# Eight routed experts and a dense feed-forward on one core: conversion of its weights shared out anew, w2 split at other places, one expert's rows turned earlier

## The chip, the cores and the metric

The kernel runs on one core of one Trainium2 chip. The metric is the device time of one execution in microseconds (us). Engines are named as in the profile: PE is the matrix engine (PEld its weight loads), DVE the vector engine, ACT the scalar engine, POOL the GpSimd engine, SP the queue that issues most DMAs.

## The reference

Three layers follow each other: a recurrent attention (mLSTM), a mixture of eight experts of which each token takes one, and a dense feed-forward with a leaky ReLU.

```python
def _attn_ref(q, k, v, i_gate, f_gate, o_gate):      # B, H, S, D = 4, 8, 768, 40
    for t in range(S):
        m_new = np.maximum(f_gate[:, :, t] + m, i_gate[:, :, t])
        f_stab = np.exp(f_gate[:, :, t] + m - m_new)
        i_stab = np.exp(i_gate[:, :, t] - m_new)
        m = m_new
        C = f_stab[:, :, None, None] * C + i_stab[:, :, None, None] * np.einsum('bhd,bhe->bhde', vt, kt)
        n = f_stab[:, :, None] * n + i_stab[:, :, None] * kt
        h_tilde = np.einsum('bhde,bhe->bhd', C, qt)
        denom = np.maximum(np.abs(np.einsum('bhd,bhd->bh', n, qt)[:, :, None]), 1.0)
        y[:, :, t] = h_tilde / denom / (1.0 + np.exp(-o_gate[:, :, t]))

def _moe_ref(x, w_gate, w1, w2):                     # 3072 tokens, 320 wide, 8 experts of 1024
    logits = x @ w_gate
    expert_idx = np.argmax(logits, axis=1)
    gate_w = softmax(logits)[np.arange(N), expert_idx]
    for e in range(E):
        mask = expert_idx == e
        out[mask] = gate_w[mask, None] * (np.maximum(x[mask] @ w1[e], 0.0) @ w2[e])

def _moe2_ref(x, w_in, w_out):                       # 320 -> 2048 -> 320
    h = x @ w_in
    return np.maximum(0.01 * h, h) @ w_out
```

## The kernel before

Every float32 product is made of fp32r products: an operand is split into a high part (a cast on ACT) and a low part (the value less the high part, on DVE or POOL), and high x high, low x high and high x low are added up in PSUM. Tiles ending in h or l are such parts (`w1h`, `w1l`, `xh`, `xl`, `hh`, `hl`).

**Stage 1** (0 to about 186 us) is the attention in chunks of 128 steps, with routing: the rows of x are scattered to a DRAM buffer `xs_d`, sorted by expert (`put_rows`, L92 to L94; an indirect DMA on POOL for each 128 tokens). The scatters are placed by a table of steps: `SC4` holds the steps of the four scatters of chunk 4; those of the last chunk follow from its routing. The expert with the most tokens is picked early and called the first (e = 0); the products of its first 256 rows (`pe`) fill the end of the stage.

**Stage 2** (186 to about 404 us) runs the eight experts, e = 0 to 7, with room for 512, 512, 472, 440, 416, 384, 364 and 320 tokens. An expert is *up* (`expert_up`, eight product groups f, each of eight products through L218, then the ReLU parts `hh` on ACT at L248 and `hl` on DVE at L249) and *down* (`expert_down`, L1409: groups a = 0, 1, 2 of 24, 24 and 16 products, each with two places k = 0, 1 behind it at which other work is put in). In the places of up f the kernel splits this expert's w2 (`split_w2`: per call ACT L186, L188 and DVE L187, L189; four calls, at f = 2, 3, 5, 6). In the places of down it prepares the next expert: the rows `xr` are loaded from `xs_d` (L236, SP) once all scatters have landed, transposed on PE (L244, `x_turn`) and split (L197 ACT, L199 DVE); w1 is split in six parts (`split_w1`: ACT L164, and L165 on DVE or POOL). `xr` can be loaded only when the numbers of tokens are sorted (`counts`, DVE); the w1 and w2 loads share two buffers `raw`, so the load of w1 for the next expert waits for the splits of w2 of this one. For e = 0 the x_turn of expert 1 stands at (a, k) = (1, 1) and (2, 1), for the others at (0, 1) and (1, 1), each time behind the side work of that place.

*Side work* is the conversion of `w_in` and `w_out`, which come as 64-bit floats and are decoded to float32 parts. It is a list of 20 `pieces` (12 of w_in, "i", quarter and row block; 8 of w_out, "o", two of the 16 blocks each); a piece has five steps (`piece_step`): t = 0 issues the stores of the piece before (ACT queue) and two DVE operations; t = 1 one on ACT; t = 2 two on DVE; t = 3 one on DVE and a cast on ACT; t = 4 two subtractions on POOL (L1282, L1283). One step is taken at each place that the tables `SA` to `SH` list (0 to 7 are f in up, 8 + 2a + k in down), one table for an expert: 7, six times 7 and 13 steps, 62 in all. The first `NPRE` pieces of w_out are stored to a DRAM buffer `wo_d` and loaded again, since their final place is a buffer that w1 holds till the last up is done; `load_wo` (L1332, POOL queue, one DMA for the high and one for the low parts) brings them in at the start of the last down.

**Stage 3** (about 404 us to the end) is the dense feed-forward: two halves of the 2048 columns, six windows of 512 tokens, 96 units i of eight products `pva` and, three units later, twelve products `poa` that read `w_out` (`wo_tiles`: blocks 0 to 7 and 14 in the buffers of w1, the others in those of w2). The first half needs blocks 0 to 7. One step of side work is taken in each unit till the pieces are done: 38 units. `windows()` (some forty small DVE operations on a table of overflow windows) stands at unit 44.

The order on every engine is the order of the code; an engine waits in that order.

Of the kernel before, what the change touches and what calls it, by code (L numbers as in the profile page):

```python
# [51 lines left out]
def tile_mlstm_moe_ffn(  # L52
# [108 lines left out]
    def split_w1(raws, ws, i, eng):  # L161
        hf, a = divmod(i, 3)
        cs = slice(hf * HF, (hf + 1) * HF)
        nc.scalar.copy(ws[0][:, a, cs], raws[hf][:, a])  # L164
        eng.tensor_tensor(ws[1][:, a, cs], raws[hf][:, a], ws[0][:, a, cs].bitcast(F32), ALU.subtract)  # L165
# [16 lines left out]
    def split_w2(raws, ws, i):  # L182
        hi, lo, mx = ws
        s = slice(2 * i, 2 * i + 2)
        raw = raws[i // 2][:, (i % 2) * 2 : (i % 2) * 2 + 2]
        nc.scalar.copy(hi[:, s], raw[:, :, 0 : 2 * P])  # L186
        nc.vector.tensor_tensor(lo[:, s], raw[:, :, 0 : 2 * P], hi[:, s].bitcast(F32), ALU.subtract)  # L187
        nc.scalar.copy(mx[:, s, 0:KR], raw[:, :, 2 * P : DM])  # L188
        nc.vector.tensor_tensor(mx[:, s, KR:P], raw[:, :, 2 * P : DM], mx[:, s, 0:KR].bitcast(F32), ALU.subtract)  # L189
# [62 lines left out]
    with ExitStack() as sx:  # L252
# [264 lines left out]
        IDLE = 8  # L517
        W2N = 2
        POOLB = 3, 0, 0, 3, 4, 6, 4, 10
        SC4 = 200, 208, 205, 213  # L520
        FILL = 8, 2, 2, 2, 6
        FR = 180, 187, 190, 192
        W1S = 185, 188, 191, 206, 206, 206
# [627 lines left out]
    def list_rows(i0, i1):  # L1151
        for i in range(i0, i1):
            put_rows(list_w, (), list_d, sm_t["posi"][:, i : i + 1], sm_t["pay"][:, i])
# [145 lines left out]
                        wo_d[hl, f0:f1].rearrange("a p d -> p a d"), t.bitcast(F32).rearrange("p (a d) -> p a d", d=DM)  # L1299
                    )  # L1300

    NPRE = 2
    wo_t, wi3 = {}, []

    def wo_tiles(nm, part):
# [12 lines left out]
        return wo_t[i, 0][:, r * DM :], wo_t[i, 1][:, r * DM :], (i, f == 14)  # L1318


    pieces = [("i", qd, a) for qd in range(NQ - 1) for a in range(3)] + [("o", f2, 0) for f2 in range(NF // 4)]
    pieces += [("i", NQ - 1, a) for a in range(3)] + [("o", f2, 0) for f2 in range(NF // 4, NF // 2)]
    side_at = [0]

    def run_side(end=5 * len(pieces)):
# [24 lines left out]
    def ffn_x(xs, w, parts=range(3), n=CAP):  # L1350
        for a in parts:
            split_x(x2T[:, a, w * CAP : w * CAP + n], a, *xs)
        return xs


    def turn_ps(nm, a):
        return pm.tile([P, CAP], F32, tag="dn" if (nm, a) == (0, 2) else "tr", name=f"pt{nm}_{a}")
# [73 lines left out]
    }  # L1431
    for i in range(24):
        extras.setdefault((2 + i // 4, 2 * (i % 4) + 1), []).append(lambda i=i: list_rows(i, i + 1))
    SA = 5, 6, 7, 8, 9, 11, 13
    SB = 0, 1, 4, 6, 9, 11, 13
    SC = SD = SE_ = SF = SG = SB
    SH = 0, 1, 3, 4, 5, 6, 7, 8, 9, 10, 11, 12, 13

    SIDE = (SA, SB, SC, SD, SE_, SF, SG, SH)

    def side_work(e, i):
        if i in SIDE[e]:
            run_side()

    for e in range(E):
        last = e + 1 == E

        def in_up(f, e=e):
            global_w2 = (w2raw, w2s)
            if e and f in (2, 3, 5, 6):  # L1450
                split_w2(*global_w2, (2, 3, 5, 6).index(f))
            side_work(e, f)
            for fn in extras.get((e, f), ()):
                fn()

        hh, hl = first_up(in_up) if e == 0 else expert_up(e, xs, w1s, in_up, CAPS[e])
        if not last:
            e_r = nc.sync.value_load(slots[0:1, 0, e + 1 : e + 2], min_val=0, max_val=E - 1)
            row = nc.sync.value_load(slots[0:1, 1, e + 1 : e + 2], min_val=0, max_val=(E - 1) * NT)
            xr = x_rows_tile(e + 1)  # L1460
            x_load(xr, row, 0, CAPS[e + 1])
            w1raw = load_w1(of_expert(w1, e_r), e + 1)
            w1n = tiles_w1(e + 1)
            xs = tiles_x(e + 1)
        else:
            xf = tiles_fx("a0")

            assert 1 <= side_at[0] - 5 * (3 * (NQ - 1) + NPRE) <= 3
            wo_tiles("a", 0)
            load_wo(0, 2 * NPRE)  # L1470
        w2u = w2s

        def in_down(a, k, e=e, last=last):
            nonlocal_w = (w1raw, w1n) if not last else None
            if last and k == 1:
                ffn_x(xf, 0, (a,))
            side_work(e, 8 + 2 * a + k)
            if k == 0:
                if not last and a < 2:
                    for i in range(3):  # L1480
                        split_w1(*nonlocal_w, 3 * a + i, nc.gpsimd if i == 2 else nc.vector)
            else:

                for t in () if last else {0: (0, 1), 1: (2,)}.get(a - (e == 0), ()):
                    x_turn(turn_ps(e + 1, t), xr, xs, t, CAPS[e + 1])

        col = nc.scalar.value_load(slots[0:1, 2, e : e + 1], min_val=0, max_val=NT)
        col_v = nc.vector.value_load(slots[0:1, 2, e : e + 1], min_val=0, max_val=NT)
        expert_down(e, hh, hl, w2u, col, col_v, in_down, CAPS[e])
        if not last:  # L1490
            w1s = w1n
            w2raw, w2s = load_w2(of_expert(w2, e_r), e + 1), tiles_w2(e + 1)
# [94 lines left out]
    def ffn_side(i, k):  # L1587
        if k == 0:
            run_side()
        if (i, k) == (4, 1):  # L1590
            load_meta()
        if (i, k) == (44, 1):
            windows()

    ffn("a", list(range(NT // CAP)), tiles_wi("a"), lambda w, n: meta[:, 4 * w + n], xf, ffn_side, parts=2)
# [78 lines left out]
```

## Time and profile before

| | |
|---|---|
| time, median of 3 runs | 767.43 us (765.39 to 768.24) |
| profiled execution | 768.0 us, of which the profile's span is 766.3 us |
| PE busy | 727.3 us, 95% |
| PEld, DVE, ACT, POOL busy | 641.8, 492.2, 372.6, 255.5 us |
| mean granted clock of PE | 0.971 of 2.4 GHz |

A busy PE is not a PE at its peak: matmuls are pipelined, and the shown duration of one overlaps the next. So the places that matter are those at which a row of PE shows idle time ahead of it (in brackets, with what ended it), and the stretches in which the granted clock is 0.50, which is the lower of its two levels, 1.2 GHz.

### The profile page before, as it was taken

To read this page: it belongs to the slowest core of one execution; us is meant where nothing else is said; L and a number is where in the kernel's file an instruction comes from. 1 tells how busy PE (TensorE), PEld (TensorE's weight loads), DVE (VectorE), ACT (ScalarE), POOL (GpSimd) and SP (SyncE) were. 2 spreads that over 40 slices of the span, in tenths; PEclk is the share of its full clock that TensorE was granted. 3 is DMA by queue.
4 is the path that set the end of the run, shared out by engine and by line. 5 is a ranking of instruction groups with operands and counts; after the bars stand their busy time and mean duration, and the time that the engine had idled before them with its cause. 6 is when DMAs were issued, how large, how long until landed. Compare 5 with 4: busy or idle time off the path is not lost.

```text
span 766.3 us, 12304 instructions
## 1 busy us (share of the span) xinstructions
PE 727.3 (95%) x4226; PEld 641.8 (84%) x4226; DVE 492.2 (64%) x1066; ACT 372.6 (49%) x817; POOL 255.5 (33%) x409
## 2 busy tenths in 40 slices
PE   8998999988999999999989999999999999999992
PEld 4786878877878889999878989999999988988992
DVE  6576777875686755878686766776565455455441
ACT  4685675643445545556444555455344344344330
POOL 7556577617231433446362111112100022022022
PEclk7998999997999999999989999999999999999997
DMA  6899575343645656677657222232112022022011
GB/s 169 251 313 288 164 211 175 100 125 112 187 116 179 144 131 179 129 169 196 174 125 168 83 97 96 69 104 70 35 36 103 1 69 69 1 69 70 0 35 38
DMA packets 62834, 92.93 MB, mean 121 GB/s; under 512 B 9839, under 2 KB 43407, under 8 KB 62767
## 3 DMA queue, kind: packets, MB, share of 16 engines
q1 hardware_dynamic: 49295, 64.54, 30.4%
q10 hardware_dynamic: 9344, 18.35, 7.6%
q0 software_dynamic: 4128, 9.20, 3.8%
q8 instruction: 35, 0.57, 0.3%
q14 instruction: 32, 0.26, 0.1%
HBM read 68.09 MB, written 23.88 MB: 120 GB/s over the span
## 4 chain that ended last, share of the span: by engine, by line
PE 41%; issue 30%; DMA 9%; DVE 8%; POOL 7%; ACT 3%; SPq 1%; ACTq 0%; POOLq 0%; DVEq 0%
PE pva L218 8%; PE pu L218 8%; PE pd L1409 7%; POOL out_dram L94 3%; DMA w1r<-in_moe_w_dram 3%; PE poa L1523 3%; PE poa L1522 3%; PE poa L1521 3%; PE pI L590 2%; PE pS L556 2%; DMA xs_d<-x,dsti 2%; DMA rdo<-in_moe_w_out_dram 1%; POOL xs_d L94 1%; DMA qB<-in_qt_dram 1%; PE pD L544 1%
## 5 line engine op out<-in xcount | busy, mean ns | idle before, releaser
L218 PE MATMUL pva<-xhfa,wi 128*128 128x512 f32 x432 | 134.2, 393 | 0.4 <-DVE xhfa L199 0.4
L1566 DVE TENSOR_TENSOR lka<-pva,lka 128x512 f32<-128x512 f32 x96 | 66.3, 691 | 86.8 <-ACT lka L1565 86.3
L1565 ACT ACTIVATE lka<-pva 128x512 f32<-128x512 f32 x96 | 57.3, 597 | 98.7 <-PE pva L218 93.1
L1569 ACT CAST gha<-lka 128x512 fp32r<-128x512 f32 x96 | 59.6, 621 | 89.6 <-DVE lka L1566 89.6
L1571 DVE TENSOR_TENSOR gla<-lka,gha 128x512 fp32r<-128x512 f32 x96 | 70.1, 730 | 50.5 <-ACT gha L1569 48.1
L218 PEld LDWEIGHTS pva<-xhfa,wi 128*128 128x128 f32 x432 | 78.2, 188 | 13.3 <-DVE xhfa L199 0.8
L94 POOL DMA_INDIRECT out_dram<-ota,meta x24 | 25.3, 1053 | 186.6 <-DVE ota L1534 183.6
L547 ACT ACTIVATE E<-pD,wn 128x128 f32<-128x128 f32 x192 | 56.1, 366 | 25.6 <-PE pD L544 20.1
L218 PE MATMUL pu<-xh,w1h 128*128 128x256 f32 (+7 forms) x192 | 65.9, 345 | 1.9 <-DVE xh L199 1.7
L1523 PE MATMUL poa<-woaw1h,gla 128*128 128x320 f32 x216 | 66.8, 309 | 0.6 <-DVE gla L1571 0.6
L1522 PE MATMUL poa<-woaw1l,gha 128*128 128x320 f32 x216 | 66.7, 309 | 0.0
L1521 PE MATMUL poa<-woaw1h,gha 128*128 128x320 f32 x216 | 66.6, 308 | 0.0
L218 PE MATMUL pu<-xh,w1l 128*128 128x256 f32 (+7 forms) x192 | 65.2, 341 | 0.0
L590 PEld LDWEIGHTS pI<-nv,P 128*128 128x128 f32 x384 | 53.1, 198 | 10.4 <-DVE P L558 4.9
L590 PE MATMUL pI<-nv,P 128*128 128x123 f32 (+1 forms) x384 | 55.5, 280 | 3.5 <-DVE P L558 3.5
L218 PE MATMUL pva<-xlfa,wi 128*128 128x512 f32 x144 | 56.1, 389 | 0.0
L556 PE MATMUL pS<-qB,nK 120*128 120x384 f32 (+1 forms) x132 | 54.8, 498 | 0.0
L1409 PE MATMUL pd<-hh,w2l 128*128 128x512 f32 (+6 forms) x128 | 46.7, 365 | 2.7 <-DVE w2l L187 2.7
L1409 PE MATMUL pd<-hl,w2h 128*128 128x512 f32 (+6 forms) x128 | 46.8, 365 | 1.0 <-DVE hl L249 1.0
L1409 PE MATMUL pd<-hh,w2h 128*128 128x512 f32 (+6 forms) x128 | 47.1, 368 | 0.0
L248 ACT ACTIVATE hh<-pu 128x256 fp32r<-128x256 f32 (+7 forms) x64 | 31.7, 501 | 29.8 <-PE pu L218 24.6
L165 POOL TENSOR_TENSOR w1l<-w1r,w1h 128x512 fp32r<-128x512 f32 x14 | 20.1, 1437 | 77.3 <-ACT w1h L164 77.3
(307 smaller groups left out, 1883.7 us busy)
## 6 DMA issues: line engine op xcount, KB each, us to landing
w2r<-in_moe_w_dram SPq DMA_DIRECT2D x16, 640.0 KB
w1r<-in_moe_w_dram SPq DMA_DIRECT2D x16, 512.0 KB
xs_d<-zr SPq DMA_DIRECT2D x16, 320.0 KB
rdo<-in_moe_w_out_dram ACTq DMA_DIRECT2D x16, 320.0 KB
w1r<-in_moe_w_dram SPq DMA_DIRECT2D x32, 128.0 KB
rdi<-in_moe_w_in_dram ACTq DMA_DIRECT2D x8, 512.0 KB
no<-in_o_gate_dram SPq DMA_DIRECT2D x12, 320.0 KB
pba<-part_d SPq DMA_DIRECT2D x6, 640.0 KB
```

The lines of the kernel that those rows point to most:

```text
L218: nc.tensor.matmul(ps_t, a, b, start=start, stop=stop)
L547: nc.scalar.activation(Et[:, j], pD[:, j], AF.Exp, bias=wn[:, c, 3, HG * g + j : HG * g + j + 1])
L556: nc.tensor.matmul(pS[:, :nh], nats["K", c][:R, g], QB[p][:R, g - GCUT[p], :nh], start=True, stop=True)
L590: nc.tensor.matmul(pI[:, r0:, j], Pt[:, j], vj, start=True, stop=True)
L1409: nc.tensor.matmul(pd, aa, bb, start=(i == 0), stop=(i == len(seq) - 1))
L1521: nc.tensor.matmul(po[n], g_h[:, tsl], woh, start=(f == f0), stop=False)
L1522: nc.tensor.matmul(po[n], g_h[:, tsl], wol, start=False, stop=False)
L1523: nc.tensor.matmul(po[n], g_l[:, tsl], woh, start=False, stop=(f == f1))
L1565: nc.scalar.activation(lk, pu, AF.Copy, scale=0.01)
L1566: nc.vector.tensor_tensor(lk, pu, lk, ALU.max)
L1569: nc.scalar.copy(g_h, lk)
L1571: nc.vector.tensor_tensor(g_l, lk, g_h.bitcast(F32), ALU.subtract)
```

## The change

`NPRE` goes from 2 to 4, so all eight w_out blocks of the first half go by way of `wo_d`, and the last quarter but one of w_in moves behind them in the list of pieces: quarters 0 and 1, w_out pieces 0 to 3, quarter 2, w_out 4 and 5, quarter 3, w_out 6 and 7. The tables take 7, five times 7, 5 and 5 steps in stage 2, 52 in all; 48 are left for the units of stage 3. `split_w2` moves to f = 0, 1, 3, 4. In down, x_turn now stands ahead of the w1 splits and of the side work, and for e = 0 at (0, 0) and (1, 0). The four scatters of chunk 4 are put at step 200. `windows()` moves to unit 53.

```diff
-        SC4 = 200, 208, 205, 213
+        SC4 = 200, 200, 200, 200
...
-    NPRE = 2
+    NPRE = 4
...
-    pieces = [("i", qd, a) for qd in range(NQ - 1) for a in range(3)] + [("o", f2, 0) for f2 in range(NF // 4)]
-    pieces += [("i", NQ - 1, a) for a in range(3)] + [("o", f2, 0) for f2 in range(NF // 4, NF // 2)]
+    pieces = []
+    for qs, f2s in ((range(NQ // 2), range(NPRE)), ((2,), (4, 5)), ((3,), (6, 7))):
+        pieces += [("i", qd, a) for qd in qs for a in range(3)] + [("o", f2, 0) for f2 in f2s]
...
+    W2F = 0, 1, 3, 4
     SA = 5, 6, 7, 8, 9, 11, 13
-    SB = 0, 1, 4, 6, 9, 11, 13
-    SC = SD = SE_ = SF = SG = SB
-    SH = 0, 1, 3, 4, 5, 6, 7, 8, 9, 10, 11, 12, 13
+    SB = 2, 5, 6, 7, 9, 11, 13
+    SC = SD = SE_ = SF = SB
+    SG = 2, 5, 6, 7, 9
+    SH = 2, 5, 6, 7, 9
...
-            if e and f in (2, 3, 5, 6):
-                split_w2(*global_w2, (2, 3, 5, 6).index(f))
+            if e and f in W2F:
+                split_w2(*global_w2, W2F.index(f))
...
             load_wo(0, 2 * NPRE)
...
+            if k == (e > 0) and not last:
+                for t in {0: (0, 1), 1: (2,)}.get(a, ()):
+                    x_turn(turn_ps(e + 1, t), xr, xs, t, CAPS[e + 1])
+            if k == 0 and not last and a < 2:
+                for i in range(3):
+                    split_w1(*nonlocal_w, 3 * a + i, nc.gpsimd if i == 2 else nc.vector)
             side_work(e, 8 + 2 * a + k)
-            if k == 0:
-                if not last and a < 2:
-                    for i in range(3):
-                        split_w1(*nonlocal_w, 3 * a + i, nc.gpsimd if i == 2 else nc.vector)
-            else:
-                for t in () if last else {0: (0, 1), 1: (2,)}.get(a - (e == 0), ()):
-                    x_turn(turn_ps(e + 1, t), xr, xs, t, CAPS[e + 1])
...
-        if (i, k) == (44, 1):
+        if (i, k) == (53, 1):
             windows()
```

What stands on PE behind the first group of the first expert's down, before (`pd_0`, `pd_1` are groups a = 0 and 1, `pt` the transposes of expert 1's rows):

```order
L1409 MATMUL pd_0_3039<-hh_7_2775,w2h_2784 128x512
L1409 MATMUL pd_0_3039<-hh_7_2775,w2l_2785 128x512
L1409 MATMUL pd_0_3039<-hl_7_2783,w2h_2784 128x512
L1409 MATMUL pd_1_3078<-hh_0_2768,w2h_2784 128x512
L1409 MATMUL pd_1_3078<-hh_0_2768,w2l_2785 128x512
```

and after:

```order
L1410 MATMUL pd_0_3039<-hh_7_2775,w2h_2784 128x512
L1410 MATMUL pd_0_3039<-hh_7_2775,w2l_2785 128x512
L1410 MATMUL pd_0_3039<-hl_7_2783,w2h_2784 128x512
L244 MATMUL pt_0_3064<-ident,xr_3007 128x128 x4
L244 MATMUL pt_1_3071<-ident,xr_3007 128x128 x4
L1410 MATMUL pd_1_3092<-hh_0_2768,w2h_2784 128x512
```

The eight transposes that stood behind group 1 now stand behind group 0.

On ACT in the last expert's up, from its first ReLU part (`hh_0`) to its fifth, before (L186 and L188 split w2, L1298 stores a converted piece):

```order
L248 ACTIVATE hh_0_5022<-pu_0_5038 128x320
L248 ACTIVATE hh_1_5023<-pu_1_5051 128x320
L1298 DMA wo_d<-d_ho_0_5013 128x2x320
L1298 DMA wo_d<-rdo_0_4629 128x2x320
L248 ACTIVATE hh_2_5024<-pu_2_5070 128x320
L186 CAST w2h_5019<-w2r_0_5015 128x512
L188 CAST w2m_5021<-w2r_0_5015 128x2x64
L248 ACTIVATE hh_3_5025<-pu_3_5085 128x320
L186 CAST w2h_5019<-w2r_0_5015 128x512
L188 CAST w2m_5021<-w2r_0_5015 128x2x64
L1250 ACTIVATE d_eo_0_5064<-d_eo_0_5064,bexp 128x640
L248 ACTIVATE hh_4_5026<-pu_4_5103 128x320
```

and after:

```order
L248 ACTIVATE hh_0_5024<-pu_0_5040 128x320
L186 CAST w2h_5021<-w2r_0_5017 128x512
L188 CAST w2m_5023<-w2r_0_5017 128x2x64
L248 ACTIVATE hh_1_5025<-pu_1_5055 128x320
L186 CAST w2h_5021<-w2r_0_5017 128x512
L188 CAST w2m_5023<-w2r_0_5017 128x2x64
L248 ACTIVATE hh_2_5026<-pu_2_5072 128x320
L1214 DMA rdi_0_5083<-in_moe_w_in_dram 128x1024
L248 ACTIVATE hh_3_5027<-pu_3_5088 128x320
L186 CAST w2h_5021<-w2r_1_5019 128x512
L188 CAST w2m_5023<-w2r_1_5019 128x2x64
L248 ACTIVATE hh_4_5028<-pu_4_5105 128x320
```

Two splits of w2 now come before the third ReLU part, and the two stores ahead of it are gone from here.

On POOL at the end of the last expert's up, before (L1282 and L1283 are the subtractions of a w_out piece, `list_d` a scatter, the last two the loads of `load_wo`):

```order
L1282 TENSOR_TENSOR d_ao_0_5065<-d_ao_0_5065,d_ho_0_5136 128x640
L1283 TENSOR_TENSOR rdo_0_4804<-d_ao_0_5065,d_eo_0_5064 128x640
L93 MEMSET gap 1x1
L94 DMA list_d<-pay,posi 3072x2
L1332 DMA woaw1h<-wo_d 128x4x320
L1332 DMA woaw1l<-wo_d 128x4x320
```

and after:

```order
L1282 TENSOR_TENSOR d_ao_0_4859<-d_ao_0_4859,d_ho_0_5132 128x640
L1283 TENSOR_TENSOR rdo_0_4778<-d_ao_0_4859,d_eo_0_4858 128x640
L93 MEMSET gap 1x1
L94 DMA list_d<-pay,posi 3072x2
L1333 DMA woaw1h<-wo_d 128x8x320
L1333 DMA woaw1l<-wo_d 128x8x320
```

The order there is the same, and each of the two loads is twice as long.

## Rows read from the trace of the kernel before

**Rows 1.** Busy time by stretch: length, PE, PEld, DVE, ACT, POOL, PEclk, DMA, GB/s.

```profile
364.70:378.20 13.50, 12.69 (x75) 11.65 (x74) 7.98 (x15) 6.27 (x14) 2.71 (x2) 1.00 0.71 165
378.20:394.80 16.60, 13.42 (x88) 12.64 (x87) 14.03 (x25) 8.46 (x20) 10.53 (x10) 1.00 0.49 140
394.80:401.60 6.80, 5.82 (x22) 5.43 (x22) 5.25 (x8) 2.49 (x4) 3.43 (x5) 0.50 0.58 102
...
417.00:550.00 133.00, 133.00 (x741) 120.38 (x740) 90.27 (x135) 66.26 (x115) 23.89 (x20) 1.00 0.25 85
```

**Rows 2.** Timeline of PE, first expert: start, duration, line, [idle before, what ended it].

```profile
190.38 0.87 PE L244 MATMUL pt<-ident,xr 128*128 128x128 f32 x6 [1.94 <-DMA xr<-xs_d]
...
215.99 0.66 PE L244 MATMUL pt<-ident,xr 128*128 128x128 f32 x4 [0.65 <-DVE xl L199]
...
219.26 0.50 PE L218 MATMUL pu<-xh,w1h 128*128 128x512 f32 x1 [1.23 <-DVE xh L199]
```

**Rows 3.** Timeline of POOL, SP and DVE around 184 to 192 us.

```profile
183.37 0.96 POOL L94 DMA_INDIRECT xs_d<-x,dsti  x1 [0.22 <-issue]
...
187.34 0.37 SPq L236 DMA_DIRECT2D xr<-xs_d  x1
...
190.22 0.28 DVE L189 TENSOR_TENSOR w2m<-w2r,w2m 128x128 fp32r<-128x128 f32 x1
...
192.05 0.43 DVE L199 TENSOR_TENSOR xh<-pt,xh 64x256 fp32r<-64x256 f32 x1
```

**Rows 4.** Timeline of PE and SP in the first expert's down.

```profile
199.70 0.40 PE L1409 MATMUL pd<-hh,w2h 128*128 128x512 f32 x1
...
201.10 0.37 SPq L236 DMA_DIRECT2D xr<-xs_d  x1
...
210.61 1.03 PE L244 MATMUL pt<-ident,xr 128*128 128x128 f32 x8
```

**Rows 5.** Timeline of ACT and PE, seventh expert's down and eighth's up.

```profile
371.23 1.66 ACT L164 CAST w1h<-w1r 128x512 fp32r<-128x512 f32 x3 [5.78 <-DMA w1r<-in_moe_w_dram]
...
374.87 0.64 PE L244 MATMUL pt<-ident,xr 128*128 128x128 f32 x3 [0.81 <-DVE xl L199]
...
379.74 0.41 PE L218 MATMUL pu<-xh,w1h 128*128 128x320 f32 x1 [0.49 <-DVE xh L199]
```

**Rows 6.** Timeline of ACT, PE, POOL and DVE, eighth expert.

```profile
384.51 0.44 ACT L248 ACTIVATE hh<-pu 128x320 fp32r<-128x320 f32 x1 [2.51 <-POOL gap L93]
...
390.93 0.41 PE L1409 MATMUL pd<-hh,w2l 128*128 128x320 f32 x1 [0.52 <-DVE w2l L187]
394.24 0.41 PE L1409 MATMUL pd<-hh,w2l 128*128 128x320 f32 x1 [2.17 <-DVE w2l L187]
396.20 0.64 PE L1409 MATMUL pd<-hl,w2h 128*128 128x320 f32 x1 [0.98 <-DVE hl L249]
...
390.72 1.58 POOL L1282 TENSOR_TENSOR d_ao<-d_ao,d_ho 128x640 f32<-128x640 f32 x1 [2.30 <-ACT d_ho L1277]
...
390.80 1.65 DVE L189 TENSOR_TENSOR w2m<-w2r,w2m 128x128 fp32r<-128x128 f32 x1
```

**Rows 7.** Groups of DVE instructions, 378.2 to 394.8: count, busy us, mean ns, idle.

```profile
L249 DVE SCALAR_TENSOR_TENSOR hl<-pu,hh 128x320 fp32r<-128x320 f32 x7 | 3.4, 485 | 0.9 <-ACT hh L248 0.9
...
L187 DVE TENSOR_TENSOR w2l<-w2r,w2h 128x512 fp32r<-128x512 f32 x4 | 2.7, 682 | 0.0
```

**Rows 8.** Timeline of POOL and PE into stage 3.

```profile
396.77 0.84 POOL L1332 DMA_DIRECT2D woaw1h<-wo_d  x1
...
409.40 1.65 PE L218 MATMUL pva<-xhfa,wi 128*128 128x512 f32 x6 [0.39 <-DVE xhfa L199]
...
412.71 0.30 PE L1521 MATMUL poa<-woaw1h,gha 128*128 128x320 f32 x1
```

**Rows 9.** DMA queues, POOL's alone: packets, MB, share; 395 to 403, 403 to 407.5 us.

```profile
q0 software_dynamic: 552, 0.65, 50.0%
...
q0 software_dynamic: 534, 0.66, 58.6%
```

More of the change, by code (lines that the diff above doesn't have):

```diff
@@ L1466, in tile_mlstm_moe_ffn @@
             xf = tiles_fx("a0")
-            assert 1 <= side_at[0] - 5 * (3 * (NQ - 1) + NPRE) <= 3
+            assert side_at[0] > 5 * (3 * NQ // 2 + NPRE)
             wo_tiles("a", 0)
```

## Prediction

> **What bounds the kernel now.** I read the busy time by stretch first. In stage 3 PE shows 133.00 us busy of 133.00 at full granted clock, with a step of side work beside most units [rows 1]; nothing can be won there, so what counts is where PE still waits between 186 and 413 us. For that I read the timeline of PE for idle time in brackets and ask of each what ended it. There are five places. **A**: the first expert's remaining rows land late, 1.94 us [rows 2]. **B**: the second expert's rows are turned so late that its up waits twice, 0.65 and 1.23 us [rows 2]. **C**: between the seventh and the eighth expert, 0.81 and 0.49 us [rows 5]. **D**: in the eighth expert's down PE waits for split w2 and for hl, 0.52, 2.17 and 0.98 us [rows 6]; after the first two the granted clock falls to 0.50 (1.2 GHz) for 6.80 us [rows 1]. **E**: at the start of stage 3, 0.39 us [rows 8]. Experts 1 to 6 show no idle of PE in their ups and downs.
>
> **The sum, part by part.** It is made against the profiled execution, 768.0 us with a span of 766.3; the 1.7 us around the span and the 0.6 by which it lies over the median stay as they are.
>
> *Scatters (A).* The last of the eight scatters is issued at 183.37, and the load that waits for all of them goes out at 187.34, 3 us after that one's end [rows 3]. POOL idles ahead of these scatters, so three of chunk 4 now go out before those of the last chunk, and the last one is bound by its own routing instead, some 2.5 us earlier. The rows then land before PE has finished the idle products ahead of the transposes, and all 1.94 us of wait could go. But DVE is next: it splits w2 until 190.22 + 0.28, and only then takes the split of x, whose last piece starts at 192.05 [rows 3]. Without the wait this piece would be done at about 191.7 in place of 192.5: gain **0.8 us** (0 if the load is no earlier, 1.94 at most).
>
> *Second expert's rows (B).* Its transposes move from 210.61 to behind group 0. The 48 products from 199.70 to 210.61 take 0.227 each [rows 4], so group 0 ends at 205.15. The rows' load is issued at 201.10 [rows 4]. For half as many rows it was 3.0 us from issue to PE [rows 2, 3]; with half more of that for the doubled size, an estimate, they are there at 205.4. Both times move with A. So PE waits 0.3 us there and the 0.65 and 1.23 go: gain **1.6 us** (0 to 1.9). What is queued behind the transposes' split on ACT are the w1 casts, whose data lands later anyway; they have two groups of down as cover.
>
> *w2 sooner (C, D).* For experts 1 to 6 it moves work between places that cost PE nothing: 0, as the same four splits and the same steps stand in an up of the same length. For the seventh: w1 of the eighth lands so late that ACT idles 5.78 us for it [rows 5], and its load waits for the buffers that the w2 splits free. These are now done two places earlier, about 2.7 us at 1.33 a place; the x split is also ahead of the side work. Both waits of C go: gain **1.3 us** (0.5 to 1.3).
>
> D: before, ACT stood 2.51 us in front of the third ReLU part, since the stores ahead of it in its queue wait for POOL [rows 6]; that pushed the w2 splits to the end of up. Now DVE has in this up eight hl (0.485 each, 3.9), four w2l (0.68, 2.7) [rows 7], four w2m (0.28 [rows 3], 1.1) and three operations of side work at about 0.85 (w2l scaled to 640 columns, an estimate, 2.6): 10.3 us. It starts about 1.7 us behind PE's first product, so it ends at 12.0. PE needs the last hl with the 22nd product of down: 64 products of up and 21 more at 0.142 (0.227 scaled to 320 columns), 12.1. That is a tie; if each w2m takes 1.65 beside a POOL subtraction [rows 6], 0 to 3 us are left. I take 0.5: of 3.67 idle, **3.2 us** go (0.7 to 3.7). With no long pause the clock should stay at 1.00: half of 6.80, **3.4 us** (0 or 3.4). For comparison, 1.94 us idle in A and 1.88 in B were followed by no fall.
>
> *Fewer steps in stage 2, more in stage 3.* Ten steps (two pieces) leave the last two experts; the chain from down to stage 3 loses the side work that delayed it on DVE: **0.4 us** in E (0 to 0.4). The ten steps come to units 38 to 47. PE is 133.00 of 133.00 busy beside the same steps [rows 1], so they cost 0; DVE (90.27 of 133) is the cover. If it were gone, the four POOL subtractions could each hold PE by 1.4 us (1.65 less 0.28), 5.5. `windows()` costs 0 in unit 53 as in unit 44: no step competes with it there.
>
> *The load of w_out (F).* This is what the change adds on the path. Count from the first product of the last up, 378.20 before; the first `poa` then started 34.5 us later [rows 8]. Less the waits of C, D, E in it and the clock (0.49, 3.67, 0.39, 3.4) it is needed at 26.6, plus the 0.5 left in D, 27.1. The loads stand on POOL behind two subtractions (1.58 each [rows 6]) that follow ACT's cast in the sixth place (about 9 us), one wait for DVE and one scatter (1.3): about 14. Before, the two loads of 0.65 MB were issued from 396.77, 552 of their packets had gone by 403 and the rest by 407.5 [rows 8, 9]: 10.7 us. Twice the bytes: at the best pace that 0.66 MB in 4.5 us with its slow start allows, some 0.36 MB a us, 3.6 us more; at the mean pace 10.7 more. So the low parts land at 28.3 to 35.4, 1.2 to 8.3 too late; with the second load started sooner behind the first, in time. I take **1.5 us lost** (0 to 8.3), near the first, since the fixed part of a load isn't doubled.
>
> The page "DMA: Bandwidth & Descriptors" of the Trainium skill, section on the anatomy of one DMA on the SWDGE path, gives 2.0 us plus the bytes over 436 GB/s for such a load, and its bandwidth table advises large ones. An estimate by it: 5.0 us each, nothing lost in F, and a sum 1.5 us better, 756.7. The trace doesn't agree with it here: by it 0.65 MB would be 3.5 us, and the first load took about 6 [rows 8, 9].
>
> Sum: 0.8 + 1.6 + 1.3 + 3.2 + 3.4 + 0.4 = 10.7 less 1.5 = **9.2 us**. From 768.0 that is 758.8, from the median 767.43 it is **758.2 us**. With all gains at their upper ends and nothing lost: 1.9 + 1.9 + 1.3 + 3.7 + 3.4 + 0.4 = 12.6, 754.8.
>
> **Rivals.**
> 1. *The w_out load holds PE for long and the clock falls.* For it: D's pauses of 2.17 and 0.52 were followed by a fall [rows 1, 6], and the loads now have little slack. A wait of 4.0 in place of 1.5, and 3.4 for the clock: 767.43 - 10.7 + 7.4 = 764.1.
> 2. *The eighth expert stays behind its conversions.* DVE had 14.03 busy of 16.60 there [rows 1]; if the w2m run long, 2.5 us of D and the fall of the clock remain: D gives 1.2 and no clock, the wait in F shrinks to 0: 767.43 - 5.3 = 762.1.
> 3. *The second expert's rows aren't there when PE turns to them.* The wait moves to group 0 and nothing of B is won: 759.8. It lies in the forecast's range.
> 4. *POOL's subtractions beside stage 3 hold PE.* Row for it: w2m 1.65 in place of 0.28 while POOL subtracts [rows 3, 6]; against: PE full beside the same steps. 5.5 us: 763.7. The page "SBUF — State Buffer" of the Trainium skill, section on its two separate sides, has DVE with two SBUF inputs and GpSimd share a port as an exclusive lock; by that rule each `gla` behind a subtraction stands still, and the row of 1.65 agrees with it.
> 5. *Slower than before.* The same place as 1: both loads run at the mean pace and DVE's lag of up to 2.2 us delays the subtractions and the store that the second load waits for. Then w_out is there at 14 + 2.2 + 21.4 = 37.6, PE waits 10.5 and the clock falls, 3.4: 13.9 lost against 10.7 won, 770.6. It decides from a wait of 7.3 us on (equal), and by half a per cent from 11.1.
>
> **How the numbers follow.** Half a per cent (3.8 us) is about what a measurement of this kernel can tell from no change; the line lies at 763.6. Forecast with rival 3 in it (754.8 to 761): 0.66. Rival 1, 0.14, half of it under 763.6. Rival 2, 0.09, most of it under. Rival 4, 0.04. Rival 5, 0.05, half of it over 771.3. Better than all my upper ends: 0.02. Faster: 0.66 + 0.02 + 0.07 + 0.06 = 0.81; slower 0.03; same 0.16. The range of eight in ten reaches from 754.5 to 764.5: it takes in all upper ends and rivals 1, 2 and 4 at their prices.
>
> **What would show it.** A: the first transposes follow the idle products with no wait for xr. B: eight transposes between groups 0 and 1 with at most half a microsecond ahead, and no idle ahead of the second up. C: no idle at the transposes of the eighth expert's rows. D: no wait for w2l in the last down, and a granted clock of 1.00 from 184 us to the tail. F: the idle ahead of the first `poa`, with POOL's queue as what ended it; zero would make the forecast 1.5 us too slow, four or more with a clock of 0.50 behind it is rival 1. Wrong altogether would be a wait of PE that is none of these: for w2r or w1r in experts 1 to 6, or for `gla` in stage 3.

## The result: 10.4 us faster, 756.6 against 767.0

| | before | after |
|---|---|---|
| median, beside each other | 767.0 us | 756.56 us (756.36 to 757.04) |
| ratio | | 0.987, 95% interval 0.985 to 0.989 |
| profiled execution, its span | 768.0, 766.3 | 757.0, 755.2 |
| PE busy | 727.3 us | 723.4 us |

The forecast was 758.2, range 754.5 to 764.5. PE's own work hardly shrank; what went is its waiting and the stretch at half clock. The busy time by stretch of the kernel after (length, PE, PEld, DVE, ACT, POOL, PEclk, DMA share, GB/s), which answers to [rows 1]: seventh expert's down, eighth's up and down, stage 3.

```profile
361.45:375.25 13.80, 13.80 (x83) 13.04 (x82) 8.03 (x13) 6.68 (x14) 7.64 (x8) 1.00 0.81 242
375.25:389.00 13.75, 13.75 (x95) 13.75 (x95) 11.46 (x22) 7.40 (x18) 6.13 (x9) 1.00 0.45 112
389.00:395.80 6.80, 6.80 (x44) 6.50 (x43) 1.97 (x4) 3.76 (x7) 2.50 (x3) 1.00 0.84 184
...
413.50:550.00 136.50, 136.50 (x761) 123.54 (x760) 91.51 (x141) 66.18 (x114) 22.68 (x16) 1.00 0.24 79
```

PE is busy without a gap through the last down, at 1.00, where 6.80 us stood at 0.50 before. DVE's 14.03 of 16.60 in the last expert have become 11.46 of 13.75. The timeline of PE in the first expert (start, duration, [idle before, what ended it]) answers to [rows 2, 4]:

```profile
188.03 0.82 PE L244 MATMUL pt<-ident,xr 128*128 128x128 f32 x6
189.71 0.39 PE L218 MATMUL pu<-xh,w1h 128*128 128x256 f32 x1 [0.86 <-ACT xh L197]
...
190.65 0.39 PE L218 MATMUL pu<-xl,w1h 128*128 128x256 f32 x1 [0.43 <-DVE xl L199]
...
203.85 0.39 PE L1410 MATMUL pd<-hl,w2h 128*128 128x512 f32 x1
204.21 1.09 PE L244 MATMUL pt<-ident,xr 128*128 128x128 f32 x8
```

No wait for `xr` is left at 188.03; of the 1.94 us, 1.29 came back as waits for `xh` and `xl`. The second expert's transposes follow group 0 at once. Two waits are new: one in the sixth expert (e = 5), where ACT stood 4.38 us at a reload that waits for a store (L1221) with a ReLU part queued behind, and one for w_out. Timelines of ACT, PE and POOL:

```profile
341.87 0.84 ACTq L1221 DMA_DIRECT2D rdo<-in_moe_w_out_dram  x2
342.75 0.49 ACT L248 ACTIVATE hh<-pu 128x384 fp32r<-128x384 f32 x1 [4.38 <-DMA wo_d<-rdo]
...
341.70 0.34 PE L1410 MATMUL pd<-hl,w2h 128*128 128x384 f32 x1
343.29 0.45 PE L1410 MATMUL pd<-hh,w2h 128*128 128x384 f32 x1 [1.25 <-ACT hh L248]
343.58 0.34 PE L1410 MATMUL pd<-hh,w2l 128*128 128x384 f32 x1
...
389.62 0.97 POOL L1333 DMA_DIRECT2D woaw1h<-wo_d  x1
391.24 0.91 POOL L1333 DMA_DIRECT2D woaw1l<-wo_d  x1 [0.64 <-DMA wo_d<-rdo]
...
402.45 0.41 PE L1524 MATMUL poa<-woaw1l,gha 128*128 128x320 f32 x1 [0.86 <-DMA woaw1l<-wo_d]
```

**Where the time went**, in every kernel of this study. Each column is worked out from starts on PE's timeline: 1, last idle product of stage 1 to first product of the first down; 2, from there to the second down; 3, sixth down to seventh up; 4, seventh up to eighth up; 5, eighth up to its down; 6, that down to stage 3; 7, to the first `poa`; 8, first to last `poa`. The second to the sixth down take 109.0 in all of them, the tail after the last `poa` 14.4 to 15.2. The total runs from the first down to the end. Stage 1 differs between executions: in the kernels that have it as the kernel after, the first down starts at 194.5 to 199.5. So parts are compared by the columns, and medians only with the median of before taken beside them.

| kernel | 1 | 2 | 3 | 4 | 5 | 6 | 7 | 8 | total |
|---|---|---|---|---|---|---|---|---|---|
| before | 11.64 | 32.83 | 12.14 | 24.53 | 10.14 | 16.41 | 7.96 | 338.80 | 566.57 |
| after | 10.80 | 30.62 | 13.87 | 23.13 | 9.38 | 9.39 | 7.28 | 339.18 | 556.61 |
| g2_after_again | 10.80 | 30.75 | 13.50 | 23.13 | 9.38 | 9.39 | 7.28 | 339.85 | 557.00 |
| g1_scatters | 10.80 | 33.17 | 12.14 | 28.41 | 9.39 | 15.12 | 8.47 | 338.98 | 569.19 |
| e1_turn | 11.32 | 30.62 | 12.14 | 23.29 | 10.18 | 16.25 | 8.09 | 338.90 | 562.92 |
| e2_old_pieces | 10.78 | 30.90 | 12.14 | 23.14 | 10.49 | 10.41 | 11.38 | 338.84 | 560.81 |
| e3_w2_late | 10.80 | 30.61 | 15.76 | 24.27 | 10.36 | 9.52 | 7.28 | 338.90 | 560.43 |
| e4_reload | 10.80 | 30.63 | 12.14 | 23.14 | 9.38 | 9.39 | 7.28 | 340.01 | 555.96 |
| e5_four_loads | 10.80 | 30.61 | 12.14 | 23.14 | 9.38 | 9.39 | 7.28 | 338.68 | 554.77 |
| e6_w2_behind | 10.59 | 31.15 | 13.31 | 23.19 | 9.39 | 9.39 | 7.28 | 339.55 | 557.24 |
| e7_list_early | 10.80 | 30.59 | 12.14 | 23.14 | 9.39 | 9.39 | 7.28 | 338.58 | 554.37 |
| g3_list_early | 10.80 | 30.62 | 12.14 | 23.14 | 9.38 | 9.39 | 7.28 | 338.64 | 554.76 |
| e8_meta_late | 10.80 | 30.69 | 12.14 | 23.14 | 9.38 | 9.39 | 7.28 | 338.77 | 554.60 |
| g4_one_split | 9.99 | 30.94 | 12.14 | 23.33 | 9.39 | 9.39 | 7.28 | 338.69 | 555.29 |

### The profile page after: what moved, and what is told of

Same layout as the page of the kernel before. It is cut to its first block, busy times and chain, and to the rows that moved or that the text cites. A ratio compares the mean times of both kernels' runs of the same rounds, so it can differ in the third digit from the quotient of the medians.

```text
span 755.2 us, 12304 instructions
## 1 busy us (share of the span) xinstructions
PE 723.4 (96%) x4226; PEld 639.9 (85%) x4226; DVE 488.4 (65%) x1066; ACT 372.3 (49%) x817; POOL 252.5 (33%) x409
## 4 chain that ended last, share of the span: by engine, by line
PE 64%; issue 15%; DMA 7%; POOL 5%; DVE 4%; ACT 1%; SPq 1%; ACTq 0%; POOLq 0%; DVEq 0%
PE pva L218 15%; PE pd L1410 12%; PE pu L218 10%; PE poa L1524 5%; PE poa L1525 5%; PE poa L1523 5%; POOL out_dram L94 3%; PE pI L590 3%; PE pS L556 3%; DMA wo_d<-rdo 2%; DMA woaw1l<-wo_d 1%; DMA no<-in_o_gate_dram 1%; PE pt L244 1%; PE pe L218 1%; DMA xs_d<-x,dsti 1%
## 5 line engine op out<-in xcount | busy, mean ns | idle before, releaser
L249 DVE SCALAR_TENSOR_TENSOR hl<-pu,hh 128x256 fp32r<-128x256 f32 (+7 forms) x64 | 35.8, 564 | 14.9 <-ACT hh L248 14.3
```

## Experiments on the parts of the change

**Transposes alone.**

```diff
 # before
+            if k == (e > 0) and not last: ... x_turn(...)      # ahead of split_w1 and side_work
```

> The kernel before with one part of the change alone: the transposes of the next expert's rows ahead of the w1 splits and of the side work, and one group sooner in the first expert. Theory: this part alone gives term B, since its wait was for the splits of x and for nothing else: the second expert's down starts about 2.2 us sooner (measured in the kernel after from the first expert's down on: 3.30 less 1.09), with no idle of PE ahead of the second up, and the two waits between the seventh and the eighth expert (0.81 and 0.49 us) shrink by part. The end of the last up stays bound by the conversions, so D and the fall of the clock stay: 767.0 less 2.2 less 0 to 0.8, that is 764.0 to 764.8. Rival: B needed the sooner scatters as well (rows not yet there when PE turns to them); then the wait stands behind group 0 of the first down and 0 to 0.5 us are won, 766.5 to 767.0.

Total 562.92, 3.65 below before: column 2 fell by 2.21, column 4 by 1.24. The median was 766.37 beside 767.73 (0.998, interval 0.995 to 1.002); the profiled execution was its fastest, so the 1.24 rest on one trace. Timeline of PE, eighth expert's down:

```profile
385.61 0.41 PE L1409 MATMUL pd<-hh,w2l 128*128 128x320 f32 x1 [0.74 <-DVE w2l L187]
388.91 0.64 PE L1409 MATMUL pd<-hh,w2l 128*128 128x320 f32 x1 [2.16 <-DVE w2l L187]
390.87 0.64 PE L1409 MATMUL pd<-hl,w2h 128*128 128x320 f32 x1 [0.53 <-DVE hl L249]
```

Busy time of the stretch behind it, with the clock (seventh column of times):

```profile
388.67:395.50 6.83, 6.06 (x21) 5.66 (x22) 5.39 (x9) 1.80 (x4) 4.23 (x5) 0.50 0.45 68
```

All of B comes from the order of the transposes, without the sooner scatters. Column 4 has 1.24 of C as well, which the forecast had put to w2; but e3 below, with the same order, has 0.26 of it, so e1 alone does not settle C. D and the half clock stay as they were.

**Scatters alone.**

```diff
 # before
+        SC4 = 200, 200, 200, 200
```

> The kernel before with one part of the change alone: the four scatters of chunk 4 at step 200. Theory: this part alone gives A and no more: the load of the first expert's rows goes out about 4 us sooner, the 1.94 us ahead of their transposes are gone, 1.29 of them come back as waits for xh and xl behind the w2 splits, and from the last product of stage 1 to the first product of the first down it takes 12.4 in place of 13.3 us; B's two waits (0.65 and 1.23), C, D and the fall of the clock stay. From the first down on it is as long as before, 566.6 us. Rival: the sooner rows also let the second expert's rows be there sooner, and part of B is won: 565 to 566.

A is there and is 0.84 us (column 1; e1, whose scatters stand as before, has 11.32 there, so the gain is 0.5 to 0.8). The total of the traced execution is 2.6 us longer, though, and the median the same as before (768.65 beside 769.69; 0.999, interval 0.997 to 1.002). Timeline of ACT and PE in the seventh expert's down; PE then ran 3.4 us at clock 0.50:

```profile
370.87 1.66 ACT L164 CAST w1h<-w1r 128x512 fp32r<-128x512 f32 x3 [7.43 <-DMA w1r<-in_moe_w_dram]
...
374.51 0.73 PE L244 MATMUL pt<-ident,xr 128*128 128x128 f32 x3 [2.46 <-DVE xl L199]
```

The load of w1 went out at the same place of the program (361.32) and took 9.55 us to that cast, 7.89 in the kernel before (from 363.34 to the cast in [rows 5]). So in this execution more was lost at a transfer (column 4, 3.88) than A won; the median shows no such loss. Neither reading had that.

**All but the moved conversions.**

```diff
 # after
-    NPRE = 4
+    NPRE = 2
+    pieces = ...          # the list of before
+    SG = SB
+    SH = 0, 1, 3, 4, 5, 6, 7, 8, 9, 10, 11, 12, 13
...                       # windows() at unit 44 again
```

> The kernel after without the moved conversions: scatters, transposes and w2 splits as in the kernel after, but the list of pieces, two pieces of w_out by way of DRAM and the 62 steps in stage 2 (13 of them in the last expert) as before. Theory: what frees the last down, and with it the granted clock, is that fewer steps and no stores stand in the last expert; then A 0.84, B 2.2 and C 1.3 to 2.2 are won, D and the clock's fall stay, the wait of expert 5's down for hh and the wait for w_out at the start of stage 3 do not arise: 767.0 less 4.3 to 5.2 gives 761.8 to 762.7, with a stretch at granted clock 0.50 behind the last down. Rival: the sooner split of w2 alone frees the last down; then all of D and the clock (7.0) are won here too, with nothing lost for expert 5 and w_out: 767.0 less 11.3 to 12.2, 754.8 to 755.7, below the kernel after.

Median 761.31 beside 767.73 (0.990, 0.987 to 0.994), near the 761.8 to 762.7 of the theory, but by another way. The sooner w2 does free the last down (column 6 from 16.41 to 10.41, no wait for `w2l` left); the loss then stands at the start of stage 3 (column 7, 7.96 to 11.38). Timeline of ACT, then of PE:

```profile
395.84 0.72 ACT L1277 CAST woaw1h<-d_ao 128x640 fp32r<-128x640 f32 x1 [2.35 <-DVE d_ao L1256]
...
397.60 0.73 PE L218 MATMUL pva<-xhfa,wi 128*128 128x512 f32 x2 [1.40 <-ACT xhfa L197]
398.86 0.77 PE L218 MATMUL pva<-xlfa,wi 128*128 128x512 f32 x1 [0.53 <-DVE xlfa L199]
```

Busy time and clock behind these waits:

```profile
398.93:402.34 3.41, 3.41 (x8) 2.74 (x9) 1.29 (x4) 1.07 (x3) 1.28 (x1) 0.50 1.57 355
```

ACT stands 2.35 us at a step of side work with the split of stage 3's rows queued behind; PE waits 1.93 and runs 3.41 us at 0.50. Columns 5 to 7 together: before 34.51, e1 34.52, here 32.28, after 26.05.

**All but the sooner w2.**

```diff
 # after
-    W2F = 0, 1, 3, 4
+    W2F = 2, 3, 5, 6      # SB 0, 1, 4, 6, 9, 11, 13; SG, SH 0, 1, 4, 6, 9
```

> The kernel after with w2 split at f = 2, 3, 5, 6 again and the side work of the ups at 0, 1, 4, 6 (in the last two experts 0, 1, 4, 6 and 9). Theory: the sooner split let the loads of w1 start sooner, and with them C was won; here C comes back, 1.3 to 2.2 us between the seventh and the eighth expert, and the wait of ACT for w1r there grows from 4.47 toward 5.78. On the wait of expert 5's down (1.25 idle ahead of a product that needs hh) two readings part: if the sooner loads of w1 delay the store that ACT's queue waits for, it is gone here (756.6 + 1.3 to 2.2 - 1.3 to 1.8: 756.1 to 757.5); if the store takes some 9 us by itself, or behind the scatters to the list, the wait stands two groups sooner in the same up and costs the same (757.9 to 758.8). The clock stays at 1.00 by both.

Median 759.79 (0.988, 0.984 to 0.991). Columns 5 to 7 are 27.16, so of the 8.46 won there 7.35 come from the moved conversions without the sooner w2. In the sixth expert the wait for the store is gone, as the first reading has it (the store out at 329.89, the reload at 333.86, the loads of w1 from 334.63 on). The time of neither reading came, though, since column 3 is worse for another reason. Timeline of ACT and PE:

```profile
345.10 1.66 ACT L164 CAST w1h<-w1r 128x512 fp32r<-128x512 f32 x3 [6.79 <-DMA w1r<-in_moe_w_dram]
...
348.13 0.53 PE L244 MATMUL pt<-ident,xr 128*128 128x128 f32 x3 [1.87 <-DVE xl L199]
```

The load of w1, issued at 334.63 behind four scatters to the list, was late: it landed 10.5 us after its issue, and from 348.70 on PE ran 3.41 us at clock 0.50. Against the kernel after the total is 3.8 longer: 1.9 in column 3, 1.1 in column 4, 1.1 in columns 5 to 7, less 0.3 in column 8.

## Experiments on the two new waits

**The reload later.**

```diff
 # after
-        if t == 2 and q > 0 and stored(q - 1) and ...
+        if t == (4 if q == 7 else 2) and q > 0 and stored(q - 1) and ...
```

> The kernel after with one load of a raw piece moved: the load into the buffer from which the first w_out piece is stored is issued two steps later (behind the fifth step of the next piece in place of its third). Theory: ACT's 4.38 us of waiting in expert 5's up for that store, with hh queued behind, is what costs PE 1.25 idle and slows the products beside it, 1.76 in all; here it is gone and nothing takes its place: 754.8 to 755.4. Rival: the gain is given back before the eighth expert, whose rows and w1 come by loads of their own pace (ACT still waits 4.47 for w1r in the seventh down): the landmarks are then 1.3 to 1.8 sooner at the seventh expert's up and equal at the eighth's, and the time is 756.6.

Median 756.18. Column 3 is 12.14 as before the change: the wait of 1.25 cost 1.73, and the place of the reload in ACT's queue was its cause. But the total fell by 0.65 alone. It was not lost where the rival had it (column 4 is unchanged). PE stood longer at the start of stage 3, 1.72 where 0.86 had been; the second row is g2_after_again, the kernel after once more:

```profile
402.54 0.41 PE L1524 MATMUL poa<-woaw1l,gha 128*128 128x320 f32 x1 [1.72 <-DMA woaw1l<-wo_d]
...
400.93 0.42 PE L1524 MATMUL poa<-woaw1l,gha 128*128 128x320 f32 x1 [1.51 <-DMA woaw1l<-wo_d]
```

This is not the gain coming back because PE came sooner: the loads of w_out go out 14.4 us behind the eighth's up in all three, so they move with PE. From the first issue to this product they took 12.8 us in the kernel after, 13.7 here and 13.5 in g2. The same kernel thus shows a wait of 0.86 or of 1.51; by these traces the later reload is worth between 0.65 and the 1.73 of column 3.

**w_out in four loads** (with the later reload).

```diff
-            load_wo(0, 2 * NPRE)
+            load_wo(0, NPRE)
+            load_wo(NPRE, 2 * NPRE)
```

> The kernel with the later reload (e4_reload), and the load of w_out at the start of stage 3 in four DMAs: high and low parts of blocks 0 to 3, then of 4 to 7. Theory: in e4_reload PE came 1.76 us sooner to stage 3 and stood 1.72 us for the low parts, since these are one load of 1.31 MB that counts as landed when its last block has; the first poa needs block 0 alone. With four loads the wait of 1.72 is gone and no later product waits, as block 4 is read four units (14 us) later: from the first product of the first down to the end 554.2 to 554.5 in place of 555.96 (after: 556.61). Rival: the wait is for the start of the loads and their slow first packets (issued at 388.9, few packets until 392.4), not for their length: then 1.0 to 1.7 of it stay, 555.2 to 556.0.

Median 753.54 beside 766.83. The wait for w_out is gone, though the last of the four loads landed as late as with two (13.0 us from the first issue); what is left is the next in line, 0.34 for `gla`. Total 554.77, against 554.2 to 554.5 expected: the 0.34 weren't in the sum.

```profile
398.25 0.42 PE L1526 MATMUL poa<-woaw1h,gla 128*128 128x320 f32 x1 [0.34 <-DVE gla L1574]
```

**The list's load out of the way** (with the later reload).

```diff
-        after(nc.sync.dma_start(meta, list_d...), list_w)
+        after(nc.scalar.dma_start(meta, list_d...), list_w)
```

> The kernel with the later reload (e4_reload), and the load of the list (meta, 3072 pieces of 8 bytes) issued on ACT's queue in the fifth unit of stage 3 in place of SP's queue, where it went out at 390.3, beside the load of w_out. Theory: from 395.5 to 400 the list's packets cut the rate of the w_out load from about 384 to about 308 KB per us; without them it lands 1.0 us sooner, so that of the 1.72 us ahead of the first poa 0.7 is left: 555.0 from the first product of the first down to the end (e4_reload 555.96). Rival: the queues are slow there whatever goes beside, or units 5 and on now wait for ACT behind the issue: 555.9 or more.

Median 752.36. The wait is 0.44 where 0.7 was expected, the total 554.60. From the first issue to this product it took 12.4 us, and 12.8 to 13.7 in the four executions with the list's load beside it (after, g2, e6, e4). A load of 24 KB in 3072 pieces of 8 bytes thus cost the 2.6 MB beside it 0.4 to 1.3 us, as far as one execution without it shows.

```profile
398.42 0.41 PE L1524 MATMUL poa<-woaw1l,gha 128*128 128x320 f32 x1 [0.44 <-DMA woaw1l<-wo_d]
```

**Scatters to the list elsewhere.**

```diff
 # after
-        extras.setdefault((2 + i // 4, 2 * (i % 4) + 1), [])...
+        extras.setdefault(((2, 3, 4, 6)[i // 6], i % 6), [])...
```

> The kernel after with the 24 scatters to the list moved: six each in experts 2, 3, 4 and 6 in place of four each in experts 2 to 7, so that none stands in the ups of experts 5 and 7. Theory: behind such scatters (rows of 8 bytes) the DMA queues stand nearly still for 2 to 3 us, and that makes the store in expert 5 (9.8 us) and the load of w_out (few packets for its first 3 us) slow. Then the store lands some 3 us or more sooner, ACT's 4.38 us of waiting and PE's 1.25 shrink to nearly nothing with the reload at its old place, and the wait of 0.86 for w_out is gone too: from the first product of the first down to the end 554.0 to 554.8 in place of 556.61. Rival: the store is slow because the loads of w1 (1.3 MB) share the queues; then expert 5 is as in the kernel after, and only w_out gains, 555.7 to 556.6.

Median 754.61 beside 766.83; total 554.37. Both new waits are gone with the reload at its old place and w_out in two loads. In the kernel after, the DMA queues behind the store (issued 332.1) and behind the scatters (to 334.5) look so (windows as above; the last three columns are PEclk, DMA share, GB/s):

```profile
331.00:334.00 3.00, 3.00 (x19) 3.00 (x18) 3.00 (x8) 1.92 (x6) 2.78 (x5) 1.00 0.68 155
334.00:337.00 3.00, 3.00 (x19) 3.00 (x18) 1.60 (x4) 1.40 (x5) 0.48 (x1) 1.00 0.66 52
337.00:341.00 4.00, 4.00 (x25) 4.00 (x24) 3.19 (x6) 1.37 (x3) 0.00 (x0) 1.00 1.01 287
```

Without scatters in that up, with the same w1 loads behind the same store (issued 329.1):

```profile
328.50:331.50 3.00, 3.00 (x20) 3.00 (x19) 2.97 (x7) 1.85 (x5) 0.00 (x0) 1.00 0.64 170
331.50:334.50 3.00, 3.00 (x19) 3.00 (x19) 2.31 (x6) 2.63 (x6) 0.00 (x0) 1.00 0.88 290
```

52 GB/s have become 290. The reload went out 6.2 us behind the store, 9.8 in the kernel after; over all executions it is 9.2 to 9.8 in three with the scatters (after, g2, e6) and 6.2 to 6.8 in three without (e7, g3, g4). So the rival, the loads of w1 alone, is out. They have a part in it, though: in e3 three scatters went out behind the store and no load of w1, and it had landed after 4.0 us at most. The wait for w_out went for two reasons: with no scatter ahead of them on POOL the loads went out 13.0 us behind the eighth's up, 1.4 sooner than in the kernel after, and they took 11.6 us in place of 12.8.

**First expert's w2 behind its rows.**

```diff
 # after
-        W2N = 2
+        W2N = 0
```

> The kernel after with all four w2 splits of the first expert behind its x_turn (two stand ahead of it in the kernel after). Theory: the 0.86 and 0.43 us that PE now waits for xh and xl are ACT and DVE still splitting w2; without them both are gone, 1.29 us from the first transposes to the first down. Rival: the split of x takes its time by itself (two transposes, a cast, a subtraction in a row) and PE comes to it at once: then 0.3 us are won at most, or the w2 parts come too late for the first down, and as much is lost there.

Median 755.06. The 1.29 are gone, but two other waits came, for `hl` in the first up and for the rows in the first down; the rival had feared a loss, but at the w2 parts (PE's timeline):

```profile
191.78 0.39 PE L218 MATMUL pu<-xh,w1h 128*128 128x256 f32 x1 [0.85 <-DVE hl L249]
201.82 1.09 PE L244 MATMUL pt<-ident,xr 128*128 128x128 f32 x8 [0.49 <-DMA xr<-xs_d]
```

Column 1 wins 0.21, column 2 loses 0.53.

## A version that is faster than both

> The kernel after once more, as the measure for the two kernels beside it: 556.6 us from the first product of the first down to the end, 755 to 758 in all, as stage 1 takes up to 2 us more or less from run to run.

> The kernel with the list's scatters in experts 2, 3, 4 and 6 (e7_list_early), in more rounds, as the version that may beat the kernel after. Theory: the wait of expert 5's down and the one for w_out are gone in every execution, 554.4 from the first product of the first down to the end, 2.2 us (0.3 per cent) faster than the kernel after. Rival: the gain of the first look came with its stage 1, which was 3 us shorter, and the medians are equal within 0.7 us.

> The kernel with the scatters moved (e7_list_early) and one of the first expert's w2 splits ahead of its x_turn in place of two. Theory: with two, PE waits 0.86 and 0.43 for xh and xl behind them; with none (e6_w2_behind) these were gone but 0.85 for hl in the first up and 0.49 for the rows in the first down came. With one, the first two shrink to 0 to 0.5 and hl is in time: 0.4 to 0.9 us are won from the first transposes to the first down (10.58 in the kernel after). Rival: what is won there returns at once as the wait for the second expert's rows in the first down, whose load's time is set by other work: 0 to 0.3.

The edit of g4 is that of e7 and `W2N = 1`. Measured beside each other and beside before (769.69 there): after 758.20 (ratio 0.985, 0.983 to 0.987), scatters moved 754.50 (0.980, 0.977 to 0.982), with one split ahead 751.12 (0.976, 0.974 to 0.978). Both beat the kernel after by more than the intervals; of the 3.7 us between the medians of the first two, the traced executions show 2.2 from the first down on (totals 557.00 and 554.76). Their stages 1 differ by 2.2 as well, though the edit doesn't touch that stage. One split ahead of the rows wins 0.81 in column 1 and loses 0.32 in column 2, and its total of 555.29 is 0.5 longer. So the traces show 0.3 at most of its further lead of 3.4 us; where the rest comes from is open. PE's timeline:

```profile
187.13 0.38 PE L218 MATMUL pu<-xh,w1h 128*128 128x256 f32 x1 [0.15 <-ACT xh L197]
187.97 0.39 PE L218 MATMUL pu<-xl,w1h 128*128 128x256 f32 x1 [0.34 <-DVE xl L199]
201.84 1.09 PE L244 MATMUL pt<-ident,xr 128*128 128x128 f32 x8 [0.29 <-DMA xr<-xs_d]
```

## Why the prediction was right, step by step

The sum forecast 9.2; the span fell by 11.05. By column:

- **A**, 0.8: measured 0.84 (0.5 to 0.8 with e1 as the measure). Next in line were ACT's part of the split, 0.86, and DVE's, 0.43; the forecast had DVE alone. Stage 1 itself ended 0.25 sooner, far less than it varies by.
- **B**, 1.6: measured 2.21. The step that was mis-sized is the wait that should take its place (0.3, and 201.10 with 4.5 is 205.6 and not 205.4; the trace has room for 0.13) and the price of a pause: 1.88 us of idle in brackets cost 2.2 of time.
- **C**, 1.3: both waits are gone, and 1.40 in column 4 and 0.76 in column 5 were won, more than the idle again. The sooner w2 is a part of the cause, not all of it. Column 4 (24.53 before, 24.27 in e3, 23.29 in e1) follows the time from the seventh's up to ACT's split of the eighth's rows: 20.2, 19.9 and 18.9 us; in the kernel after, at 17.7, PE no longer waits for it. This split stands behind the first casts of w1, after the change too (only for e = 0 does x_turn stand ahead of the w1 splits). The new order takes a step of side work from between the two, 0.6 to 0.7 us; the rest is when w1 lands, counted from the same up: 0.7 sooner than before in e1, 0.4 later in e3, and 1.8 sooner in the kernel after, where w2 is split sooner. Start of the split on ACT before, in e1, in e3 and after:

```profile
373.88 0.74 ACT L197 CAST xh<-pt 128x320 fp32r<-128x320 f32 x2
...
368.27 0.76 ACT L197 CAST xh<-pt 128x320 fp32r<-128x320 f32 x2
...
372.78 0.75 ACT L197 CAST xh<-pt 128x320 fp32r<-128x320 f32 x2
...
369.84 0.75 ACT L197 CAST xh<-pt 128x320 fp32r<-128x320 f32 x2
```

- **D with the clock**, 6.6: measured 7.02 in column 6, clock at 1.00 from 184 us to the tail. The size is right by luck in part. The 3.4 for the clock counts 0.98 twice: PE is busy for 5.82 of the 6.80 us [rows 1], the rest is the wait for `hl` that stands in the 3.67 already, and half of 5.82 is 2.91. Against that, the 0.5 of wait that should stay didn't, and the pauses cost 0.44 more than their idle. DVE was done when worked out (last `hl` 12.1 behind the first product of up), but it was no tie: that `hl` is read by the 24th product, not the 22nd, which came at 12.75. Timelines of DVE and PE:

```profile
386.52 0.87 DVE L249 SCALAR_TENSOR_TENSOR hl<-pu,hh 128x320 fp32r<-128x320 f32 x2
...
388.00 0.31 PE L1410 MATMUL pd<-hl,w2h 128*128 128x320 f32 x1
```

  The forecast put D to the sooner w2. Of the 8.46 in columns 5 to 7, e3 has 7.35 by the moved conversions without it, and e2 has 2.23 by it without them.
- **E**, 0.4: measured 0.68.
- **F**, 1.5 lost: the wait was 0.86, in g2 1.51; column 8 grew by 0.38, in g2 by 1.05, since 0.59 for `gla` had stood there before. The load landed 27.2 behind the first product of up, by the forecast 28.3, and was needed at 26.3, by the forecast 27.1. The pace of 0.36 MB a us behind the slow start, for which the forecast gave no row, is borne out by e8: 370 GB/s from 392 to 396 us.
- **Steps moved to stage 3**, 0: column 8 less its idle is 338.24 in e7 and 338.21 before, so rival 4 lost nothing. The long DVE operations that it feared are there: beside a POOL subtraction a `gla` took up to 2.00 us in place of 0.69, but no idle of PE follows. Timeline of DVE in e7:

```profile
465.54 0.69 DVE L1573 TENSOR_TENSOR gla<-lka,gha 128x512 fp32r<-128x512 f32 x1
...
468.04 2.00 DVE L1573 TENSOR_TENSOR gla<-lka,gha 128x512 fp32r<-128x512 f32 x1 [0.69 <-ACT gha L1571]
```

- **Experts 1 to 6**, 0: this step failed. The list of moved work counted steps and not what a step of that kind waits for: the store and reload of a w_out piece, which before stood only in the last expert, came to the sixth, and 1.73 us were lost there (1.36 in g2). The prediction had named a wait in experts 1 to 6 as what would be wrong, but only for w2r or w1r.

2.21 + 1.40 + 0.76 + 7.02 + 0.68 + 0.84 + 0.25 less 1.73 and 0.38 is 11.05. The change's gains were 12.9 in place of 10.7 and its losses 2.1 in place of 1.5; a missed loss and undersized gains hid each other, so that the total is nearer than its parts.

On the load: by the Trainium skill's page "DMA: Bandwidth & Descriptors" (anatomy of one DMA, SWDGE path) 1.31 MB would take about 5.0 us, an estimate. Where no scatter and no list stands beside them (e7), the two took 8.0 and 8.5 us from issue to landing. They overlap, as the second went out 3.1 us behind the first, so the pair is the fairer measure: 11.6 us, by that estimate 8.1. Beside both (e6) they took 8.4 and 11.6; the measurement decides. The DMA issues of e7 (KB, and us from issue to landing):

```profile
woaw1h<-wo_d POOLq DMA_DIRECT2D x1, 1280.0 KB, 8.0
woaw1l<-wo_d POOLq DMA_DIRECT2D x1, 1280.0 KB, 8.5
```

## What to carry to other kernels

When work is moved between stages, list for each moved step not only what it costs but what it waits for, and what is queued behind it on its engine: here a reload behind a store held the ReLU. An idle time in brackets is the lower end of what a pause costs: the wait of 1.25 cost 1.73, as the product behind it started 1.59 us after the one ahead (0.17 is the rule there), and the next ones followed at 0.29. A wait that is taken away may come back in part at the next transfer, as in g4, where 0.81 was won and 0.32 came back at the second expert's rows. And before a loss is put down to such a shift, look at the same transfer in a second execution of the same kernel: the wait for w_out was 0.86 in one and 1.51 in the other.

## What the hardware showed that was not expected

- Scatters of 8-byte rows slow what stands beside them far beyond their bytes: 52 GB/s for 3 us in place of 290, and 9.2 to 9.8 us in place of 6.2 to 6.8 for a store of 0.33 MB beside the w1 loads. It is mutual: four such scatters beside the w1 loads took a median of 8.7 us to land in e6_w2_behind, one with no w1 load beside it 2.6. Why is open; no run here separates the DRAM side from the queues.
- The w1 load took 7.89 us in the kernel before and 9.55 in g1_scatters, with the same scatters at the same distance ahead of it. How long a load beside such a neighbour takes thus differs by over 1 us between executions, and a margin of 1 us behind it is none.
